# SwiGLU feed-forward on one core: the order of the first loads and of the first matrix products

## The chip, the cores and the metric

The kernel runs on one core of one Trainium2 chip. The metric is the device time of one execution in microseconds (us). Before the change three runs gave 120.45, 120.72 and 120.46 us, a median of 120.46 us. The engines of the core are named as in its profile: PE is the matrix engine (its weight loads have a lane of their own, PEld), ACT is ScalarE, DVE is VectorE, POOL is GpSimd, and SP is SyncE, which here only issues DMAs. A name with a q behind it (SPq, ACTq) is that engine's sequencer, which reads the engine's instructions in order and issues its DMAs.

## The reference

For 2048 tokens of width 512 and a hidden width of 1376, everything in bf16:

```
g = silu(x @ w_gate)      # x: 2048 x 512, w_gate: 512 x 1376
u = x @ w_up              # w_up: 512 x 1376
out = (g * u) @ w_down    # w_down: 1376 x 512
```

## The kernel before, in words

The tokens are cut into four chunks of 512 (`SC`), the hidden width into ten tiles of 128 columns and a last one of 96; such a tile is called an F tile here. The width of 512 is four slices of 128, over which each product is accumulated.

**What PE computes.** The products need x with its width on the partitions (`xT_sb`). For each chunk and F tile there are two groups of matmuls: a gate group (kind G) and an up group (kind U), each of four matmuls of 128 x 128 weights against 512 tokens, into a PSUM bank of its own. ACT reads the gate group's bank and writes silu of it, DVE multiplies that by the up group's bank and writes the hidden tile `hT_sb`. The odd last F tile is done in groups X and Y. When all chunks are done, groups of kind O multiply the hidden tiles by `w_down`, and the results are copied and stored. Groups use the eight PSUM banks in turn, in the order in which they are planned.

**The start.** x comes in by two ways. The first 256 tokens (`HT`) are loaded plainly into `xn_sb`, PE transposes them in eight transposes (four groups of kind T, line 346), and DVE and ACT each copy two of the four banks into `xT_sb`. The second 256 tokens of chunk 0, named `x0b`, come by a transposing DMA (line 87), as do chunks 1 to 3. Ahead of the transposes PE runs warming matmuls on constants (`warm`, line 337): `N_WARM` = 6 of 512 columns and `N_FILL` = 2 of 128 columns. They compute nothing.

Because x0b is late, the first groups are cut in two. PE runs the gate and the up group of F tiles 0 and 1 on the first 256 tokens (the very first two groups in steps of 128 tokens), and then the same four groups on the second 256 tokens. All later groups run on 512 tokens at once.

**The loads.** The weights come in slabs of F tiles (`slabs`): 0, 1, 2 to 3, 4 to 6, and 7 to the end; a slab is one DMA for gate and one for up (`load_w`, line 92). The two queues that issue them are ACT's and SP's. ACT issues gate 0 and up 0, and only then comes its first activation, on a dummy of 4 columns (line 269), ahead of which its table is loaded. SP issues, in this order, x's first half (line 108), gate 1, up 1, the transposing x0b, the slabs from F tile 2 on, a small piece of up (`wut`), the transposing loads of chunks 1 to 3, and the pieces of `w_down`. Each load has a semaphore of its own, and PE waits for it where it first needs the load (`need`). Each of the engines takes its instructions in the order written; PE's order is written out by hand in `on_tensor`.

Of the kernel before, what the change touches and what calls it, by code (L numbers as in the profile page):

```python
# [4 lines left out]
ACT = mybir.ActivationFunctionType  # L5
# [1 line left out]
BF16 = mybir.dt.bfloat16  # L7
FP32 = mybir.dt.float32

N_WARM = 6  # L10
N_FILL = 2


def bass_standalone__swiglu_ffn__prompt_kernel(nc, x, w_gate, w_up, w_down, out):
    _, S, D = x.shape
    F = w_gate.shape[1]
    P = 128
    KD = D // P
    NFF = F // P
    NFT = NFF + 1  # L20
# [8 lines left out]
    HT = SC // 2  # L29
# [10 lines left out]
    UPH = F + 32  # L40
# [4 lines left out]
    with ExitStack() as es:  # L45
# [12 lines left out]
        adummy = sb("act_dummy", [P, 8], FP32)  # L58
# [18 lines left out]
        def load_sem(name):  # L77
            loads[name] = sem(f"s_{name}")
            return loads[name]
# [3 lines left out]
        zero_c = nc.const_aps.tensor(0.0, [P, 4], FP32)  # L83


        def load_x(eng, name, t0, t1):
            eng.dma_start_transpose(
                xT_sb[:, :, t0:t1], xf[t0:t1, :]
            ).then_inc(load_sem(name), 16)

        def load_w(eng, name, src, base, f0, f1):
            eng.dma_start(
                w_sb[:, :, base + f0:base + f1],
                src[:, f0:f1].rearrange("(k p) f -> p k f", p=P),
            ).then_inc(load_sem(name), 16)

        slabs = [(0, 1), (1, 2), (2, 4), (4, 7), (7, NFT)]
        slab_of = {ft: a for a, b in slabs for ft in range(a, b)}

        def load_slab(eng, a, b):  # L100
            load_w(eng, f"wg{a}", w_gate, 0, a * P, min(b * P, F))
            load_w(eng, f"wu{a}", w_up, UPH, a * P, min(b * P, F - 32))

        def loads_on_scalar(act):
            load_slab(act, *slabs[0])

        def loads_on_sync(sp):
            sp.dma_start(
                xn_sb[:, :, :].rearrange("p j d -> p (j d)"), xf[0:HT, :].rearrange("(p j) d -> p (j d)", j=NXN)
            ).then_inc(load_sem("xn"), 16)  # L110
            load_slab(sp, *slabs[1])
            load_x(sp, "x0b", HT, SC)
            for a, b in slabs[2:]:
                load_slab(sp, a, b)
            load_w(sp, "wut", w_up, F - (F - 32), F - 32, F)
            for c in range(1, NSC):
                load_x(sp, f"x{c}", c * SC, (c + 1) * SC)
            sp.dma_start(
                wd_sb[:, 0:NFF, :], w_down[0:NFF * P, :].rearrange("(k p) d -> p k d", p=P)
            ).then_inc(load_sem("wd"), 16)  # L120
            for c in range(NSC):
                sp.dma_start(
                    wdt_sb[R * c:R * (c + 1), :, :], w_down[NFF * P:F, :].rearrange("(q p) d -> p q d", p=R)
                ).then_inc(load_sem(f"wdt{c}"), 16)
            sp.dma_start(wdl_sb[:, :], w_down[NFF * P:F, LASTA:D]).then_inc(load_sem("wdl"), 16)
# [3 lines left out]
        groups = []  # L129
# [3 lines left out]
        def add_group(kind, **what):  # L133
            g = dict(kind=kind, at=len(groups), bank=banks[len(groups) % NB], readers=[], **what)
            groups.append(g)
            return g
# [30 lines left out]
        def yblk(c):  # L167
            return (0, 64) if c % 2 == 0 else (64, 128)
# [39 lines left out]
        for i in range(NXN):  # L208
            for h, eng in enumerate("DA"):
                g = add_group("T", i=i, h=h)  # L210
                op = add_op(
                    eng, g, kind="copy", out=xT_sb[:, 2 * h:2 * h + 2, i * P:(i + 1) * P],
# [3 lines left out]
        NT = len(groups)  # L216
# [11 lines left out]
        for at in range(NST):  # L228
# [5 lines left out]
            for c0, c1 in halves:  # L234
                g = add_group("O", t=t, c0=c0, c1=c1, c=c)
                if c0 == 0:
                    quads[j].append(g)
                else:
# [3 lines left out]
                    eng, g, kind="copy", out=o_sb[ob][:, c0:c1], src=g["bank"][:, 0:c1 - c0],  # L242
# [22 lines left out]
            ).then_inc(s_I, 1)  # L265

        def on_scalar(act):
            loads_on_scalar(act)
            act.activation(adummy[:, 0:4], zero_c, ACT.Silu)  # L269
            for op in act_ops:  # L270
                act.wait_ge(s_P, op["g"]["at"] + 1)
                if op["kind"] == "silu":
                    if op["free"]:
                        act.wait_ge(s_D, op["free"])
                    fn = ACT.Silu
                else:
                    if op["stored"][1]:
                        act.wait_ge(*op["stored"])
                    fn = ACT.Copy
                act.activation(op["out"], op["src"], fn).then_inc(s_A, 1)  # L280
# [15 lines left out]
        def on_tensor(pe):  # L296
            landed = set()

            def need(name):
                if name not in landed:  # L300
                    pe.wait_ge(loads[name], 16)
                    landed.add(name)
# [3 lines left out]
            def after(eng, n):  # L306
                if n > read[eng]:
                    pe.wait_ge(s_A if eng == "A" else s_D, n)
                    read[eng] = n

            def free(g):
                if g["at"] >= NB:
                    for eng, n in groups[g["at"] - NB]["readers"]:
                        after(eng, n)

            def gu_matmuls(g, n0, n1):
                c, ft = g["c"], g["ft"]
                if c > 0:
                    need(f"x{c}")
                if c == 0 and n1 > HT:  # L320
                    need("x0b")
                need(("wg" if g["kind"] == "G" else "wu") + str(slab_of[ft]))
                col = (0 if g["kind"] == "G" else UPH) + ft * P
                for dk in range(KD):
                    if c == 0 and dk % 2 == 0:
                        for i in range(n0 // P, min(n1 // P, NXN)):
                            after(*xt_ready[i, dk // 2])
                    ins = pe.matmul(  # L328
                        g["bank"][:, n0:n1], lhsT=w_sb[:, dk, col:col + P],
                        rhs=xT_sb[:, dk, c * SC + n0:c * SC + n1], start=(dk == 0), stop=(dk == KD - 1),  # L330
                    )
                if n1 == SC:
                    ins.then_inc(s_P, 1)

            def warm(n, width):
                for i in range(n):
                    pe.matmul(banks[NB - 1][:, 0:width], lhsT=ones_w, rhs=ones_m[:, 0:width], start=True, stop=True)  # L337

            warm(N_WARM, SC)
            warm(N_FILL, P)  # L340
            pe.wait_ge(s_J, 1)
# [4 lines left out]
                    ins = pe.transpose(tview(g["bank"])[:, k, :], xn_sb[:, g["i"], dk * P:(dk + 1) * P], ident[:, :])  # L346
                ins.then_inc(s_P, 1)

            g0, u0, g1, u1 = groups[NT:NT + 4]
            for g in (g0, u0):  # L350
                gu_matmuls(g, 0, P)
                gu_matmuls(g, P, HT)
            gu_matmuls(g1, 0, HT)
            gu_matmuls(u1, 0, HT)
            for g in (g0, u0, g1, u1):
                gu_matmuls(g, HT, SC)

            for g in groups[NT + 4:]:
                kind = g["kind"]
                if kind == "O":  # L360
                    break
                free(g)
                if kind in "GU":
                    gu_matmuls(g, 0, SC)
                elif kind == "X":
                    c = g["c"]
                    need(f"wg{slab_of[NFF]}")
                    need("wut")
                    for dk in range(KD):
                        ins = pe.matmul(  # L370
                            g["bank"][:, :], lhsT=w_sb[:, dk, XC0:XC0 + P],
                            rhs=xT_sb[:, dk, c * SC:(c + 1) * SC],
                            start=(dk == 0), stop=(dk == KD - 1),
                        )
                    ins.then_inc(s_P, 1)
                elif kind == "Y":
                    need(f"wu{slab_of[NFF]}")
                    for dk in range(KD):
                        for c in (2 * g["pi"], 2 * g["pi"] + 1):
                            y0, y1 = yblk(c)  # L380
                            ins = pe.matmul(  # L381
                                g["bank"][y0:y1, :], lhsT=w_sb[:, dk, YC0:YC0 + 64],
                                rhs=xT_sb[:, dk, c * SC:(c + 1) * SC],
                                start=(dk == 0), stop=(dk == KD - 1),
                                tile_position=(0, y0), skip_group_check=True,
                            )
                    ins.then_inc(s_P, 1)
# [48 lines left out]
        on_sync(nc.sync)  # L436
        on_gpsimd(nc.gpsimd)
        on_scalar(nc.scalar)
        on_tensor(nc.tensor)
        on_vector(nc.vector)  # L440

# [27 lines left out]
```

## Time and profile before

| what | value |
|---|---|
| median of three runs | 120.46 us |
| the profiled execution, its own time | 120.32 us |
| its span | 118.9 us |
| PE busy | 115.4 us, 97% |
| PE weight loads busy | 54.1 us, 45% |
| DVE busy | 47.3 us, 40% |
| ACT busy | 31.0 us, 26% |
| moved by DMA | 8.84 MB |

Times in the trace count from the span's start. A row of the timeline gives an instruction's start and its duration, the engine, the line of the kernel, the operation, what it writes and reads, how many instructions were merged into the row, and in brackets how long the engine had been idle and what ended that. The row of a DMA on a sequencer (SPq, ACTq) is the issuing alone; when its data is there is told by the table of issues, which gives for each kind of DMA the time from the start of the issue to the landing.

### The profile page before, as it was taken

Reading aid. Unit: us, or ns where it says so; the run is one execution under the profiler, and the core shown is the slowest. Engines: PE = TensorE matmul, PEld = TensorE weight load, DVE = VectorE, ACT = ScalarE, POOL = GpSimd, SP = SyncE. Lnnn points to the kernel's source line nnn. Section 1 sums busy time; section 2 is a strip of 40 time slices with the busy share of each in tenths; the row PEclk is TensorE's granted clock in tenths of the full one; section 3 lists DMA queues with packets and bytes.
Section 4 is the critical chain, followed back from the end, with each engine's and each line's share of the span. In section 5 each row is a group of like instructions: output and inputs, shape, how many; then the busy total and the mean of one; then the engine's idle time right before and its main releaser. Section 6 shows DMA issues by size and latency. Waiting matters only on the chain.

```text
span 118.9 us, 1519 instructions
## 1 busy us (share of the span) xinstructions
PE 115.4 (97%) x600; PEld 54.1 (45%) x611; DVE 47.3 (40%) x73; ACT 31.0 (26%) x53; POOL 0.4 (0%) x5
## 2 busy tenths in 40 slices
PE   7999999999999999999999999999999999999993
PEld 2774444444444444444444444344434444444452
DVE  0133443353443444433444334469617422006530
ACT  4344324454234363244262343230000000000001
POOL 1000000000000000000000000000000000000000
PEclk9999999999999999999999999999999999999999
DMA  3999999970000000000000000000004221002412
GB/s 103 271 307 357 264 162 242 328 183 24 0 0 0 6 0 0 0 3 3 0 0 0 6 0 0 0 0 0 0 0 138 88 88 44 0 0 75 145 50 88
DMA packets 17559, 8.84 MB, mean 74 GB/s; under 512 B 10640, under 2 KB 17424, under 8 KB 17552
## 3 DMA queue, kind: packets, MB, share of 16 engines
q1 hardware_dynamic: 16496, 8.48, 26.7%
q10 hardware_dynamic: 1056, 0.26, 1.0%
q8 instruction: 5, 0.08, 0.3%
q14 instruction: 2, 0.02, 0.1%
HBM read 4.81 MB, written 2.10 MB: 58 GB/s over the span
## 4 chain that ended last, share of the span: by engine, by line
PE 97%; issue 1%; DVE 0%
PE bank L328 58%; PE bank L394 29%; PE bank L370 3%; PE bank L337 2%; PE bank L408 2%; PE bank L381 2%; PE bank L346 1%; DVE o_sb L293 0%; PE bank L431 0%
## 5 line engine op out<-in xcount | busy, mean ns | idle before, releaser
L328 PE MATMUL bank<-xT_sb,w_sb 128*128 128x512 bf16 (+2 forms) x338 | 69.7, 364 | 0.4
L328 PEld LDWEIGHTS bank<-xT_sb,w_sb 128*128 128x128 bf16 x344 | 32.8, 98 | 36.4 <-issue 0.2
L289 DVE TENSOR_TENSOR hT_sb<-sg_sb,bank 128x512 bf16<-128x512 f32 x40 | 27.5, 688 | 40.5 <-PE bank L328 36.6
L394 PE MATMUL bank<-wd_sb,hT_sb 128*128 128x512 bf16 (+2 forms) x166 | 34.5, 366 | 0.4 <-issue 0.3
L280 ACT ACTIVATE sg_sb<-bank 128x512 f32<-128x512 f32 x40 | 23.8, 596 | 40.8 <-PE bank L328 40.8
L394 PEld LDWEIGHTS bank<-wd_sb,hT_sb 128*128 128x128 bf16 x170 | 16.1, 98 | 19.1 <-issue 1.3
L293 DVE CAST o_sb<-bank 128x512 bf16<-128x512 f32 (+1 forms) x16 | 10.1, 663 | 22.0 <-PE bank L408 12.3
L280 ACT ACTIVATE o_sb<-bank 128x384 bf16<-128x384 f32 x1 | 0.5, 492 | 37.8 <-PE bank L394 37.8
L289 DVE TENSOR_TENSOR ht_sb<-sgy_sb,bank 32x512 bf16<-32x512 f32 x8 | 5.5, 684 | 0.2
L289 DVE TENSOR_TENSOR ht_sb<-sgx_sb,bank 32x512 bf16<-32x512 f32 x4 | 2.8, 691 | 3.5 <-ACT sgx_sb L280 3.5
L370 PE MATMUL bank<-xT_sb,w_sb 128*128 128x512 bf16 x15 | 4.1, 379 | 0.1
L337 PE MATMUL bank<-const-bfloat16-1.0 128*128 128x512 bf16 (+1 forms) x8 | 2.9, 545 | 0.8 <-PEq L454 0.8
L280 ACT ACTIVATE sgx_sb<-bank 32x512 f32<-32x512 f32 x4 | 2.4, 588 | 4.5 <-PE bank L370 4.5
L408 PE MATMUL bank<-wdt_sb,ht_sb 32*128 32x512 bf16 (+1 forms) x48 | 2.9, 372 | 0.0
L370 PEld LDWEIGHTS bank<-xT_sb,w_sb 128*128 128x128 bf16 x16 | 1.6, 98 | 1.9
L280 ACT ACTIVATE sgy_sb<-bank 64x512 f32<-64x512 f32 x4 | 2.4, 590 | 0.1
L337 PEld LDWEIGHTS bank<-const-bfloat16-1.0 128*128 128x128 bf16 x8 | 1.0, 136 | 2.4 <-issue 2.4
L381 PE MATMUL bank<-xT_sb,w_sb 128*64 128x512 bf16 x16 | 1.9, 382 | 0.0
L408 PEld LDWEIGHTS bank<-wdt_sb,ht_sb 32*128 32x128 bf16 x48 | 1.1, 93 | 1.7 <-issue 0.8
L269 ACT ACT_TABLE_LOAD x1 | 1.3, 1283 | 1.8 <-issue 1.8
L293 DVE COPY xT_sb<-bank 128x256 bf16<-128x256 bf16 x2 | 0.6, 292 | 2.7 <-PE bank L346 2.7
L381 PEld LDWEIGHTS bank<-xT_sb,w_sb 128*64 128x64 bf16 x16 | 0.8, 109 | 1.0 <-DVE hT_sb L289 0.4
(14 smaller groups left out, 4.0 us busy)
## 6 DMA issues: line engine op xcount, KB each, us to landing
out_dram<-o_sb SPq DMA_DIRECT2D x15, 128.0 KB, 1.7
wd_sb<-in_w_down_dram SPq DMA_DIRECT2D x1, 1280.0 KB, 9.2
w_sb<-in_w_gate_dram SPq DMA_DIRECT2D x1, 480.0 KB, 5.9
w_sb<-in_w_up_dram SPq DMA_DIRECT2D x1, 448.0 KB, 6.5
w_sb<-in_w_gate_dram SPq DMA_DIRECT2D x1, 384.0 KB, 4.5
w_sb<-in_w_up_dram SPq DMA_DIRECT2D x1, 384.0 KB, 5.1
wdt_sb<-in_w_down_dram SPq DMA_DIRECT2D x4, 96.0 KB, 7.5
xn_sb<-in_x_dram SPq DMA_DIRECT2D x1, 256.0 KB, 2.8
```

Source lines behind the costliest of these rows:

```text
L269: act.activation(adummy[:, 0:4], zero_c, ACT.Silu)
L280: act.activation(op["out"], op["src"], fn).then_inc(s_A, 1)
L289: ins = dve.tensor_tensor(op["out"], op["a"], op["b"], ALU.mult)
L293: ins = dve.tensor_copy(op["out"], op["src"])
L328: ins = pe.matmul(g["bank"][:, n0:n1], lhsT=w_sb[:, dk, col:col + P], rhs=xT_sb[:, dk, c * SC + n0:c * SC + n1], start=(dk == 0), stop=(dk ...
L337: pe.matmul(banks[NB - 1][:, 0:width], lhsT=ones_w, rhs=ones_m[:, 0:width], start=True, stop=True)
L346: ins = pe.transpose(tview(g["bank"])[:, k, :], xn_sb[:, g["i"], dk * P:(dk + 1) * P], ident[:, :])
L370: ins = pe.matmul(g["bank"][:, :], lhsT=w_sb[:, dk, XC0:XC0 + P], rhs=xT_sb[:, dk, c * SC:(c + 1) * SC], start=(dk == 0), stop=(dk == KD - 1),
L381: ins = pe.matmul(g["bank"][y0:y1, :], lhsT=w_sb[:, dk, YC0:YC0 + 64], rhs=xT_sb[:, dk, c * SC:(c + 1) * SC], start=(dk == 0), stop=(dk == ...
L394: ins = pe.matmul(g["bank"][:, 0:c1 - c0], lhsT=hT_sb[:, fk, t * P:(t + 1) * P], rhs=wd_sb[:, fk, c0:c1], start=(start and fk == 0), stop= ...
L408: ins = pe.matmul(g["bank"][:, 0:c1 - c0], lhsT=ht_sb[R * c:R * (c + 1), q, j * P:(j + 1) * P], rhs=wdt_sb[R * c:R * (c + 1), q, c0:c1], s ...
```

## The change

- ACT's dummy activation, and with it the load of its table, now stands ahead of ACT's DMAs. ACT then issues up 0, up 1, gate 2 and up 2 (four DMAs of 128 KB each).
- SP issues x's first half, gate 0, gate 1, the transposing x0b, and then the slabs from F tile 3 on. It issues as many DMAs as before.
- The slabs are 0, 1, 2, 3 to 4, 5 to 7, 8 to the end.
- `N_EARLY` = 3: the groups of F tiles 0, 1 and 2 run on the first 256 tokens, then all six on the second 256. The third tile's groups are planned as ninth and tenth behind the four transposing groups and so use banks 0 and 1 again; PE waits with `free` for the copies that read them.
- One warming matmul of 512 columns less (`N_WARM` 5).

```diff
-N_WARM = 6
+N_WARM = 5
 N_FILL = 2
+N_EARLY = 3
...
-        slabs = [(0, 1), (1, 2), (2, 4), (4, 7), (7, NFT)]
+        slabs = [(0, 1), (1, 2), (2, 3), (3, 5), (5, 8), (8, NFT)]
...
         def loads_on_scalar(act):
-            load_slab(act, *slabs[0])
+            load_w(act, "wu0", w_up, UPH, 0, P)
+            load_w(act, "wu1", w_up, UPH, P, 2 * P)
+            load_slab(act, *slabs[2])
 
         def loads_on_sync(sp):
...
-            load_slab(sp, *slabs[1])
+            load_w(sp, "wg0", w_gate, 0, 0, P)
+            load_w(sp, "wg1", w_gate, 0, P, 2 * P)
             load_x(sp, "x0b", HT, SC)
-            for a, b in slabs[2:]:
+            for a, b in slabs[3:]:
                 load_slab(sp, a, b)
...
         def on_scalar(act):
+            act.activation(adummy[:, 0:4], zero_c, ACT.Silu)
             loads_on_scalar(act)
-            act.activation(adummy[:, 0:4], zero_c, ACT.Silu)
...
-            g0, u0, g1, u1 = groups[NT:NT + 4]
-            for g in (g0, u0):
-                gu_matmuls(g, 0, P)
-                gu_matmuls(g, P, HT)
-            gu_matmuls(g1, 0, HT)
-            gu_matmuls(u1, 0, HT)
-            for g in (g0, u0, g1, u1):
+            early = groups[NT:NT + 2 * N_EARLY]
+            for i, g in enumerate(early):
+                free(g)
+                if i < 2:
+                    gu_matmuls(g, 0, P)
+                    gu_matmuls(g, P, HT)
+                else:
+                    gu_matmuls(g, 0, HT)
+            for g in early:
                 gu_matmuls(g, HT, SC)
 
-            for g in groups[NT + 4:]:
+            for g in groups[NT + 2 * N_EARLY:]:
```

## The prediction

> **What bounds the kernel now.** I read the page first: the busy shares, then the chain that ended last.
>
> ```profile
> span 118.9 us, 1519 instructions
> PE 115.4 (97%) x600; PEld 54.1 (45%) x611; DVE 47.3 (40%) x73; ACT 31.0 (26%) x53; POOL 0.4 (0%) x5
> ...
> PE 97%; issue 1%; DVE 0%
> ```
>
> The chain of waits is PE's own work from 0.77 us to the end. Nothing in this change alters the arithmetic, so only the head can move: how early PE does useful work, and what it waits for until about 10 us. A delay there goes through to the end whole, because PE never idles later. So next I read the timeline of the first 10 us.
>
> ```profile
> 0.73 0.46 ACTq L92 DMA_DIRECT2D w_sb<-in_w_gate_dram  x1
> 0.74 0.40 SPq L108 DMA_DIRECT2D xn_sb<-in_x_dram  x1
> 0.77 2.93 PE L337 MATMUL bank<-const-bfloat16-1.0 128*128 128x512 bf16 x8 [0.77 <-PEq L454]
> ...
> 1.20 0.41 SPq L92 DMA_DIRECT2D w_sb<-in_w_gate_dram  x1
> 1.22 0.53 ACTq L92 DMA_DIRECT2D w_sb<-in_w_up_dram  x1
> ...
> 1.66 0.50 SPq L92 DMA_DIRECT2D w_sb<-in_w_up_dram  x1
> 1.78 1.28 ACT L269 ACT_TABLE_LOAD   x1 [1.78 <-issue]
> ...
> 2.20 1.69 SPq L87 DMA_TRANSPOSE xT_sb<-in_x_dram  x1
> ...
> 3.08 0.20 ACT L269 ACTIVATE act_dummy<-const-float32-0.0 128x4 f32<-128x4 f32 x1
> 3.29 0.15 PEld L337 LDWEIGHTS bank<-const-bfloat16-1.0 128*128 128x128 bf16 x1 [0.28 <-issue]
> 3.60 0.63 PEld L346 LDWEIGHTS bank<-ident,xn_sb 128*128 128x128 bf16 x8 [0.16 <-issue]
> ...
> 4.44 1.81 PEld L328 LDWEIGHTS bank<-xT_sb,w_sb 128*128 128x128 bf16 x24 [0.21 <-issue]
> ...
> 6.42 7.47 PEld L328 LDWEIGHTS bank<-xT_sb,w_sb 128*128 128x128 bf16 x44 [0.17 <-DMA xT_sb<-in_x_dram]
> ```
>
> The weight loads show the starts of PE's steps: transposes at 3.60, gate 0 at 4.44, the second 256 tokens at 6.42. Only the last start is put down to a DMA. Third, the table of issues, for when each load is there:
>
> ```profile
> xn_sb<-in_x_dram SPq DMA_DIRECT2D x1, 256.0 KB, 2.8
> ...
> w_sb<-in_w_gate_dram ACTq DMA_DIRECT2D x1, 128.0 KB, 3.2
> w_sb<-in_w_gate_dram SPq DMA_DIRECT2D x1, 128.0 KB, 3.4
> w_sb<-in_w_up_dram ACTq DMA_DIRECT2D x1, 128.0 KB, 3.7
> w_sb<-in_w_up_dram SPq DMA_DIRECT2D x1, 128.0 KB, 3.7
> ```
>
> Start of issue plus time to landing: x 0.74 + 2.8 = 3.5; gate 0 0.73 + 3.2 = 3.9; gate 1 1.20 + 3.4 = 4.6; up 0 1.22 + 3.7 = 4.9; up 1 1.66 + 3.7 = 5.3; x0b 2.20 + 4.2 = 6.4 (4.2 is its own row). PE's weight loads first need them at 4.44 (gate 0), 5.00 (up 0), 5.45 (gate 1), 5.83 (up 1), 6.27 (x0b). So x ends the warming, up 0 is 0.1 us ahead of its use, and x0b is 0.1 us behind.
>
> **The change part by part.**
>
> *One warming matmul less.* Warming weight loads come 0.43 us apart (the last at 2.86 and 3.29), so the warming ends at about 3.12 instead of 3.55. What is late next is x, which lands at 3.5. The packets tell what can move it: x's first packets run from 1.78 us and its last ends at 3.15; ACT's gate 0 joins from 2.50 and from there x's last third crawls. Afterwards up 0 joins in gate 0's place if ACT issues at once. Then x lands at 3.4 to 3.5, and the 0.43 us turn into waiting: gain 0, at the best 0.1. If ACT issues late, x has the engines to itself, would end near 2.65 at its first rate (60 KB per 0.2 us) and land near 3.0.
>
> *Does ACT issue at once?* No row of before has a DMA behind an ACT activation. The nearest: ACT's sequencer passed a semaphore instruction at 23.07, 0.01 us after the activation at 23.06 began, with another (23.67) still queued between; it runs ahead of its engine. POOL too starts instructions of 0.10 us each 0.03 us apart. The table load itself could be an exception. Bounds for ACT's first DMA: 0.8 and 0.73 + 1.28 + 0.20 = 2.2. I take 0.8, the rows that show a sequencer at work.
>
> [...]
>
> *Gate 0 moves behind x on SP.* It takes gate 1's place in the queue (1.20), with ACT's queue beside it as then: landing 4.6 instead of 3.9, needed 4.44. Gate 0's first load moves to about 4.62. Part comes back: before, its eight loads took 5.00 - 4.44 = 0.56 us, since the copies of the transposes ended up to 4.88; at 0.056 us each they need 0.45. So up 0 starts at 5.07 instead of 5.00: **+0.07**.
>
> *Up 0, gate 1, up 1.* Up 0 takes gate 0's place in ACT's queue (3.9 to 4.0, needed 5.07): hidden behind gate 0. Up 1 takes up 0's place (4.9 to 5.0, needed 5.95): hidden behind gate 1's matmuls. Gate 1 takes up 1's place on SP: 5.3, needed 5.52; but ACT's queue, empty from 4.5 us before, now carries 256 KB more through that time. Bounds 0 and 0.15 (half of the rate for the last 66 KB at some 55 KB per 0.2 us); nearest to the row of 5.3, I take **+0.05**.
>
> *F tile 2 from ACT, 256 tokens first.* Gate 2 and up 2 are issued at about 1.9 and 2.4, against 3.94 and 4.56 from SP before (landed 7.2 and 8.0). A half group of four matmuls takes 4 x 0.109 = 0.437 us, so PE's needs are now: up 0 5.07, gate 1 5.57, up 1 6.01, gate 2 6.44, up 2 6.88, x0b 7.32. By bytes, at 260 KB per us from 1.78 and 0.4 us to the signal, x, six weight tiles and x0b (1280 KB) are all there at 1.78 + 4.92 + 0.4 = 7.1; gate 2 earlier, about 6.0; up 2 6.6 to 6.9. I take no wait; bounds 0 and +0.25, if up 2 or x0b is last of them. Running tile 2 in halves costs 16 matmuls of 0.109 in place of 8 of 0.216: **+0.02**. The wait for x0b goes: the loads at 6.157 and 8.074 enclose 17 steps, 1.92 us where 17 x 0.109 = 1.86: **-0.06**. Banks 0 and 1 were copied out by 4.88: free.
>
> *ACT's table* is loaded by 2.2 instead of 3.28 and needed at 4.22: hidden both ways. *SP's later queue:* as many issues at the same places; slab 3 to 4 has the same 1536 KB through it as before through up 2 (8.0), needed at 9.8: hidden.
>
> *The sum:* 0 + 0.07 + 0.05 + 0.02 - 0.06 = +0.08 us. The profiled execution took 120.32 us (span 118.9, 1.4 around it), 0.14 under the median 120.46. So 120.40 for a like profile and **120.54** as a median.
>
> **The rivals.** Some 0.3% (0.36 us) is what a measurement here can tell from no change.
>
> *ACT's queue is held by the table load (slower).* Its DMAs start at 2.2: up 0 lands at 2.2 + 3.2 to 3.7 = 5.4 to 5.9, and up 2, issued at about 3.9, by the bytes ahead of it (with slab 3 to 4 beside it) between 7.0 and 8.0. PE takes up 2 last of the early groups: 0.44 for it and 24 x 0.109 = 2.62 for the second halves, so the next tile starts at 10.1 to 11.1 instead of 9.69: +0.4 to +1.4, middle 0.9: 121.4. It decides as soon as ACT's first DMA starts later than about 1.4 us, which brings up 0 behind 5.07. For it: no row shows a DMA behind a table load. Against it: the sequencer that runs ahead.
>
> *The clock rises later (slower).* Eight transposes run at 0.107 apart until 4.0 and 0.056 after; the granted clock's record starts at 4.02, 3.27 us after the first warming matmul. A gap of 0.4 us at 3.12 is new. If the count began again at 3.5, the clock would rise at 6.8, and 2.2 us of matmuls from 4.6 on would run at half speed: +1.1, 121.6. Against it: 2.9 of those 3.27 us stay busy.
>
> [...]
>
> *x is really earlier (faster).* If x lands at 3.0 and gate 0 right behind it at 4.0, and up 0 still by 4.75, transposes start 0.43 earlier; cold they take longer (eight at 0.107), so up 0 starts about 0.28 earlier. With the wait for x0b and the splitting: -0.32; with nothing lost, -0.43 - 0.06 + 0.02 = -0.47. 120.0 to 120.15. It needs ACT's loads out of x's way and yet early, between the two bounds.
>
> **How the numbers follow.** No wait by ACT, the sum above: 0.41, of which 0.05 lie above +0.36 (both upper bounds, 0.15 + 0.25, met). ACT held: 0.31. Clock: 0.09. x earlier: 0.19, of which 0.03 and the small gains stay within 0.3%, 0.16 beyond it. So faster 0.16, same 0.39, slower 0.45. The likeliest single case is the sum, own range 120.3 to 120.9. The range over the cases reaches from the fast case's 120.0 to 121.5, inside the held queue's +0.4 to +1.4; above it and below it about 0.2 are left.
>
> **What would show it.** ACT's first DMA at about 0.8 beside its table load (right), or behind 2.0 (held). The warming ending at 3.1 and the first transpose at 3.5 (right) or 3.1 (x earlier). Gate 0's first load at 4.6, put down to the DMA of w_sb. No wait for x0b ahead of the second halves at 7.3 to 7.5. The next tile (line 328, 512 tokens) at 9.8. Matmuls of 128 columns 0.056 apart from 4.6 on; at 0.107 the clock was late. Everything behind it shifted evenly; if the end moves by another amount than the third tile's end, the prediction is wrong in a place that I took as untouched.

## The result

The changed kernel takes 121.2 us (median of 121.05 to 121.38, four runs) against 120.45 for the kernel before (120.35 to 120.72, four runs beside it): a ratio of 1.0053, with a 95% interval of 1.0027 to 1.0078. It is slower, by half a per cent. The profiled execution took 121.05 us with a span of 119.7. The ratios here and below leave out executions more than 1.5% above the fastest of their kernel (three, in one experiment), and they are not quotients of the medians shown, from which they differ by up to 0.14%.

From here on "tile 2" is F tile 2, "gate 2" and "up 2" its two loads, and "landed" means the start of the issue plus the time to landing, counted from the span's start.

### The profile page after: what moved, and what is told of

It reads as the page before. It is cut to its first block, busy times and chain, and to the rows that moved or that the text cites. A ratio compares the mean times of both kernels' runs of the same rounds, so it can differ in the third digit from the quotient of the medians.

```text
span 119.7 us, 1535 instructions
## 1 busy us (share of the span) xinstructions
PE 116.0 (97%) x607; PEld 55.5 (46%) x618; DVE 47.3 (39%) x73; ACT 31.1 (26%) x53; POOL 0.4 (0%) x5
## 4 chain that ended last, share of the span: by engine, by line
PE 94%; DMA 3%; issue 1%; SPq 0%; DVE 0%
PE bank L332 58%; PE bank L400 29%; DMA w_sb<-in_w_gate_dram 3%; PE bank L376 3%; PE bank L414 2%; PE bank L387 2%; SPq L111 0%; DVE o_sb L297 0%; PE bank L437 0%
## 5 line engine op out<-in xcount | busy, mean ns | idle before, releaser
L332 PEld LDWEIGHTS bank<-xT_sb,w_sb 128*128 128x128 bf16 x352 | 34.3, 100 | 35.6 <-DMA w_sb<-in_w_gate_dram 0.3
L376 PEld LDWEIGHTS bank<-xT_sb,w_sb 128*128 128x128 bf16 x16 | 1.6, 98 | 1.9
L350 PE MATMUL bank<-ident,xn_sb 128*128 128x128 bf16 x8 | 1.0, 308 | 0.4 <-DMA xn_sb<-in_x_dram 0.4
```

Source lines behind the costliest of these rows:

```text
L332: ins = pe.matmul(g["bank"][:, n0:n1], lhsT=w_sb[:, dk, col:col + P], rhs=xT_sb[:, dk, c * SC + n0:c * SC + n1], start=(dk == 0), stop=(dk ...
L376: ins = pe.matmul(g["bank"][:, :], lhsT=w_sb[:, dk, XC0:XC0 + P], rhs=xT_sb[:, dk, c * SC:(c + 1) * SC], start=(dk == 0), stop=(dk == KD - 1),
```

## The profile after

ACT and SP in the first 3 us of the changed kernel (timeline: start, duration, engine, line, operation):

```profile
0.73 1.28 ACT L272 ACT_TABLE_LOAD   x1 [0.73 <-PEq L460]
0.74 0.39 SPq L111 DMA_DIRECT2D xn_sb<-in_x_dram  x1
...
0.79 1.01 ACTq L93 DMA_DIRECT2D w_sb<-in_w_up_dram  x2
...
1.19 0.97 SPq L93 DMA_DIRECT2D w_sb<-in_w_gate_dram  x2
...
1.83 0.53 ACTq L93 DMA_DIRECT2D w_sb<-in_w_gate_dram  x1
...
2.20 1.80 SPq L88 DMA_TRANSPOSE xT_sb<-in_x_dram  x1
...
2.39 0.53 ACTq L93 DMA_DIRECT2D w_sb<-in_w_up_dram  x1
```

ACT's sequencer issues its DMAs beside the table load, from 0.79 us on, not behind it. PE's weight loads in the same execution:

```profile
3.60 0.78 PEld L350 LDWEIGHTS bank<-ident,xn_sb 128*128 128x128 bf16 x8 [0.59 <-issue]
...
4.72 6.28 PEld L332 LDWEIGHTS bank<-xT_sb,w_sb 128*128 128x128 bf16 x59 [0.35 <-DMA w_sb<-in_w_gate_dram]
```

The transposes start at 3.60, exactly as before: x landed at 3.49 again, and the dropped warming matmul became waiting. Gate 0 starts at 4.72 instead of 4.44. Tile 3's second weight load, which starts with its first matmul, stands at 9.91 in the profile before and at 10.69 here, 0.78 later. The end moved by about as much (0.81, span 118.92 to 119.72), so the whole loss lies in the head.

Two things differ in that head, and this pair of profiles cannot tell them apart. First the loads: gate 2 landed at 6.37, up 2 at 7.57 and x0b at 7.78, where x0b had landed at 6.38. The issues of the changed kernel up to 4.5 us (KB each, median us to landing):

```profile
w_sb<-in_w_up_dram ACTq DMA_DIRECT2D x3, 128.0 KB, 3.7
...
w_sb<-in_w_gate_dram ACTq DMA_DIRECT2D x1, 128.0 KB, 4.5
xT_sb<-in_x_dram SPq DMA_TRANSPOSE x1, 5.6
```

x0b took 5.6 us from its issue, against 4.2 before. (The row of three up loads has a median of 3.7, but the third of them, up 2, took 5.2.) Second, PE's clock: the matmuls of 128 columns ran 0.107 us apart until 6.1 us, where before they came 0.056 apart from 4.0 on. The groups of PE between 4.7 and 6.1 us show it in the mean of 307 ns, against 220 ns in the profile before:

```profile
L332 PE MATMUL bank<-xT_sb,w_sb 128*128 128x128 bf16 x14 | 1.6, 307 | 0.1
```

## The experiments

Three theories stood at the start. *Clock*: the shorter warming leaves a gap in PE's work, which puts the clock's rise off. *Loads*: tile 2's loads from ACT come ahead of or beside x0b, and PE, which takes its groups in a fixed order, waits for up 2. *Gate*: gate 0's late landing on SP is the loss.

### The warming put back

```diff
-N_WARM = 5
+N_WARM = 6        # in the changed kernel
```

> The changed kernel with its sixth warming matmul put back; all else as changed. Three theories stand. CLOCK: the shorter warming leaves PE idle from 3.1 to 3.6 us, which puts the rise of its clock off from 4.0 to about 6.1, and that is the whole +0.75. LOADS: four loads ahead of x0b on ACT's queue and three on SP's make up 2 land at 7.6, so the second halves cannot begin before about 8.0; that alone is worth +0.7, and the slow clock lies beside it. GATE: gate 0 lands at 4.68 behind x on SP instead of 3.93, and that shift is the loss. Clock expects 120.6: matmuls 0.056 apart from 4.0 on and 0.55 to 0.6 saved. Loads expects about 121.1: matmuls 0.056 apart from 4.0 on, but then a wait of about 0.65 for up 2 from 6.95 to 7.6, and the next tile no earlier than 10.6. Gate expects 121.2, unchanged.

Measured: 121.12 us against 120.61, ratio 1.0033 (1.0010 to 1.0057). The loss stays. The profiled execution took 121.59 and shows the slow clock until 6.2 us although the gap was closed, so in this execution it was late without a gap. PE's weight loads, with the wait that the Loads theory needs:

```profile
4.60 2.84 PEld L332 LDWEIGHTS bank<-xT_sb,w_sb 128*128 128x128 bf16 x28 [0.26 <-DMA w_sb<-in_w_gate_dram]
8.15 1.86 PEld L332 LDWEIGHTS bank<-xT_sb,w_sb 128*128 128x128 bf16 x18 [0.71 <-DMA w_sb<-in_w_up_dram]
```

PE waits 0.71 us for up 2, which landed at 8.11.

### The shorter warming alone

```diff
-N_WARM = 6
+N_WARM = 5        # in the kernel before
```

> The kernel before with one warming matmul less and nothing else. Clock expects PE's matmuls of 128 columns to stay 0.107 apart until about 6, gate 1 at 6.1 to 6.2 instead of 5.45, the wait for x0b gone, and 121.0 to 121.1. Loads and Gate expect no change, 120.45, since x lands at 3.5 as before.

Measured: 120.53 against 120.61, ratio 1.0001 (0.9976 to 1.0025). The ten executions lie between 120.21 and 121.29, those of the kernel before beside it between 120.23 and 121.24: the same spread with the same lower end. If the gap always put the clock off, none could have taken 120.21. The Clock theory falls, as far as it ties the clock to the warming.

### Tile 2 back on SP

```diff
-N_WARM = 5
-N_EARLY = 3
+N_WARM = 6
+N_EARLY = 2
-            load_slab(act, *slabs[2])
...
-            for a, b in slabs[3:]:
+            for a, b in slabs[2:]:
```

> The changed kernel with six warming matmuls, F tile 2 loaded by SP behind x0b and run on 512 tokens (N_EARLY 2); the table first, and gate 0 and gate 1 on SP, up 0 and up 1 on ACT, stay. Loads expects x0b back near 6.4 and 120.45 to 120.6, what is left being gate 0's late landing (0.07 to 0.28). Gate expects most of the loss to stay: 120.9 to 121.2. Clock expects 120.5, as for any kernel with six warming matmuls.

Measured: 120.76 against 120.61, ratio 1.0003 (0.9979 to 1.0026). x0b landed at 6.45. The table first, gate 0 and gate 1 on SP and up 0 and up 1 on ACT cost nothing that these runs can tell. The Gate theory falls, and the loss is bound to what was taken out: tile 2 on ACT and its early groups.

### Tile 2 on ACT, gate 0 early

```diff
-            load_w(act, "wu0", w_up, UPH, 0, P)
-            load_w(act, "wu1", w_up, UPH, P, 2 * P)
+            load_slab(act, *slabs[0])
             load_slab(act, *slabs[2])
...
-            load_w(sp, "wg0", w_gate, 0, 0, P)
-            load_w(sp, "wg1", w_gate, 0, P, 2 * P)
+            load_slab(sp, *slabs[1])     # and N_WARM 6
```

> Six warming matmuls, table first, ACT issues gate 0, up 0, gate 2 and up 2, SP issues x, gate 1, up 1, x0b: so gate 0 is early and the clock in time, and only tile 2's loads from ACT with its half groups ahead of x0b are left of the change. Loads expects up 2 near 7.6 and x0b near 7.8 and about 121.1. Clock and Gate expect 120.45.

Measured: 121.05 against 120.61, ratio 1.0025 (1.0007 to 1.0043). Here the clock rose at 4.7 and gate 0 landed at 3.96, and the loss is there nevertheless. PE's weight loads:

```profile
5.15 1.76 PEld L330 LDWEIGHTS bank<-xT_sb,w_sb 128*128 128x128 bf16 x22 [0.19 <-ACT xT_sb L282]
7.42 0.66 PEld L330 LDWEIGHTS bank<-xT_sb,w_sb 128*128 128x128 bf16 x7 [0.52 <-DMA w_sb<-in_w_up_dram]
```

PE is ready for up 2 at 6.9 and waits until 7.42 (up 2 landed at 7.38). This is the Loads theory's wait, by itself.

### The two halves of it: loads alone, order alone

The loads of the change with PE's order of before:

```diff
-N_WARM = 5
-N_EARLY = 3
+N_WARM = 6
+N_EARLY = 2
```

> The changed kernel's loads (table first; up 0, up 1, gate 2 and up 2 from ACT; gate 0, gate 1, x0b from SP) with six warming matmuls and PE's order of before, two tiles early. What is open is which half of the loss belongs to the loads and which to PE's order. If the 256 KB of tile 2 ahead of x0b are a cost in themselves, x0b lands at 7.6 to 7.8 as in the changed kernel, PE waits for it from about 6.4, the next tile after the third starts at 11.2 instead of 9.9, and the time is 121.6 to 121.9, worse than the change. If the order alone (up 2 ahead of the second halves) is the cost, 120.6.

Measured: 121.9 against 120.5, ratio 1.0120 (1.0089 to 1.0151). The last of PE's waits:

```profile
7.96 2.94 PEld L332 LDWEIGHTS bank<-xT_sb,w_sb 128*128 128x128 bf16 x23 [1.27 <-DMA xT_sb<-in_x_dram]
```

And the order of the change with tile 2 from SP behind x0b:

```diff
-N_WARM = 5
+N_WARM = 6
-            load_slab(act, *slabs[2])
...
-            for a, b in slabs[3:]:
+            for a, b in slabs[2:]:
```

> The other half: six warming matmuls, tile 2 loaded by SP behind x0b (x0b near 6.4 as before), but three tiles run early, so PE takes up 2 ahead of the second halves. If the order is a cost in itself, PE waits for gate 2 (about 7.1) and up 2 (about 7.7) while x0b lies there since 6.4, the second halves start near 8.2, and the time is 121.2 to 121.7. If only the loads cost, 120.6.

Measured: 121.11 against 120.5, ratio 1.0047 (1.0025 to 1.0070), a little under what the order theory expected. The two waits:

```profile
6.95 0.33 PEld L331 LDWEIGHTS bank<-xT_sb,w_sb 128*128 128x128 bf16 x4 [0.45 <-DMA w_sb<-in_w_gate_dram]
7.49 3.60 PEld L331 LDWEIGHTS bank<-xT_sb,w_sb 128*128 128x128 bf16 x32 [0.21 <-DMA w_sb<-in_w_up_dram]
```

x0b lay there from 6.45, but PE's order asks for gate 2 (6.90) and up 2 (7.45) first. Each half is a loss by itself. Together (1.0033, the run with the warming put back) they lose less than the loads alone (1.0120): the third tile's early groups hide most of x0b's delay, and what is left is the wait for up 2.

### The kernel before, once more

> The kernel before, unchanged, profiled once more. The profiles so far have PE's clock rising at 4.0 (before), 6.1 (changed), 6.1 (six warming matmuls put back), 4.7, 5.5 and 6.6, with no regard to the warming. If that rise differs from execution to execution of one program, this one will have it at another place than 4.02, anywhere from 4 to 7.4, and its time goes with it: about 120.3 plus 0.36 for each us that the rise is later. If the rise belongs to the program, it is 4.0 again and 120.3.

The kernel is that of before, unchanged. Measured: 121.13 us, where the profile before took 120.32. PE's groups between 4.5 and 6.4 us, first of the profile before, then of this one:

```profile
L328 PE MATMUL bank<-xT_sb,w_sb 128*128 128x128 bf16 x16 | 1.2, 220 | 0.1
```

```profile
L328 PE MATMUL bank<-xT_sb,w_sb 128*128 128x128 bf16 x16 | 1.9, 308 | 0.0
```

The same 16 matmuls ran slower (308 ns each against 220), and the first of 256 columns behind them at half the rate (6.22 to 6.44, 0.21 us where it takes 0.11 later), until about 6.5 us. Tile 3's first load came at 10.48 instead of 9.69, 0.79 later; the time is 0.81 longer. So the clock's rise wanders between executions of one program: 4.0 and 6.5 in the kernel before, 6.8 with its warming shortened, 4.6 to 6.2 in the others shown here up to this point. That 7.4 is the latest, as the expectation has it, is shown by no run; in the next one the rise was at 9.9. The chip of the first profile is not on record, but on the chip of the second alone 19 executions of this kernel spread from 120.20 to 121.14.

### x0b right behind x

```diff
-N_EARLY = 3
+N_EARLY = 1
-            load_w(act, "wu0", w_up, UPH, 0, P)
-            load_w(act, "wu1", w_up, UPH, P, 2 * P)
-            load_slab(act, *slabs[2])
+            load_slab(act, *slabs[0])
+            load_slab(act, *slabs[1])
...
-            load_w(sp, "wg0", w_gate, 0, 0, P)
-            load_w(sp, "wg1", w_gate, 0, P, 2 * P)
...
-            for a, b in slabs[3:]:
+            for a, b in slabs[2:]:       # N_WARM 6, slabs of before
```

> An attempt at a version better than both: x0b is issued by SP right behind x; ACT loads its table first and then issues gate 0, up 0, gate 1, up 1; tile 2 comes from SP as before; only tile 0 runs early on 256 tokens (N_EARLY 1), then its second halves, then whole tiles. By the bytes, x0b would land by 6, ahead of its need at about 5.4 to 6.2. Loads expects PE to wait 0 to 0.5 for x0b, and gains of 0.06 (x0b's wait of before) and 0.02 (eight split matmuls fewer) if it lands in time: 120.4 to 120.9, against about 120.5.

Measured: 121.33 against 120.5, ratio 1.0064 (1.0043 to 1.0085): worse than the kernel before and no better than the change (1.0053). x0b landed at 6.08, hardly earlier for its place in the queue, and up 0, now beside it, at 6.19 instead of 4.9:

```profile
6.23 2.69 PEld L329 LDWEIGHTS bank<-xT_sb,w_sb 128*128 128x128 bf16 x18 [0.91 <-DMA w_sb<-in_w_up_dram]
```

In this profiled execution, of 123.13 us, the clock rose only at 9.9; three of eleven executions took 123.1 to 123.3. That a wait of 0.91 us causes this was not tried, and the landings and the wait shown are those of this one execution.

### Half the dose

```diff
-N_WARM = 5
-N_EARLY = 3
+N_WARM = 6
+N_EARLY = 2
-            load_slab(act, *slabs[2])
+            load_w(act, "wg2", w_gate, 0, 2 * P, 3 * P)
...
+            load_w(sp, "wu2", w_up, UPH, 2 * P, 3 * P)
             for a, b in slabs[3:]:
```

> Half the dose of the run with tile 2's loads alone: ACT issues up 0, up 1 and gate 2, and up 2 goes to SP behind x0b; six warming matmuls, two tiles early. With none of tile 2 on ACT x0b landed at 6.45 and the time was within 0.1 of the kernel before; with both halves, 256 KB, at 7.92 and 121.9. If x0b's landing goes by the bytes ahead of it, 128 KB bring it to 7.1 to 7.3 and the time to 121.1 to 121.3. If it goes by the number of queued loads on ACT or by the second of them alone, x0b stays near 6.5 or goes to 7.9.

Measured: 121.08 against 120.5, ratio 1.0034 (1.0018 to 1.0051). x0b landed at 6.98, a little ahead of the 7.1 to 7.3 expected, and PE's last wait is

```profile
7.03 4.02 PEld L333 LDWEIGHTS bank<-xT_sb,w_sb 128*128 128x128 bf16 x28 [0.33 <-DMA xT_sb<-in_x_dram]
```

So 0, 128 and 256 KB of tile 2 on ACT put x0b at 6.45, 6.98 and 7.92. At the 280 GB/s that the profile before shows between 5.0 and 5.6 us, 128 KB take 0.47 us (an estimate): the first step, 0.53, is near that, the second, 0.94, is twice as long.

### Up 1 on ACT

```diff
-N_EARLY = 3
+N_EARLY = 2
-            load_w(act, "wu0", w_up, UPH, 0, P)
+            load_slab(act, *slabs[0])
             load_w(act, "wu1", w_up, UPH, P, 2 * P)
-            load_slab(act, *slabs[2])
...
-            load_w(sp, "wg0", w_gate, 0, 0, P)
...
-            for a, b in slabs[3:]:
+            for a, b in slabs[2:]:       # N_WARM 6, slabs of before
```

> A second attempt at a version better than both: ACT loads its table first, then issues gate 0, up 0 and up 1; SP issues x, gate 1, and x0b one place earlier (at 1.7 instead of 2.2); slabs, six warming matmuls and two early tiles as before. The same 768 KB stand ahead of x0b or beside it, so x0b should land at 6.2 to 6.4 and PE's wait for it, 0.06 at the most, go: 120.4 to 120.5 against 120.5, the same within 0.3%. If an earlier place in its queue is worth as much as the bytes, x0b lands by 5.9 and up 1 at 5.9 to 6.2, and PE waits for up 1 instead: 120.5 to 120.8.

Measured: 121.51 against 120.5, ratio 1.0073 (1.0048 to 1.0099). Both guesses were wrong. With not one byte more ahead of x0b than in the kernel before, x0b landed at 7.36 and up 1 at 7.57 (5.33 before). PE's wait, and two rows of the stretches of time (us, the busy time of each engine, the clock, the DMA engines' busy share, GB/s; the clock column reads 1.00 here although PE's matmuls of 128 columns stand 0.107 us apart until 6.1, so in this document the clock is read from their spacing):

```profile
7.61 3.38 PEld L330 LDWEIGHTS bank<-xT_sb,w_sb 128*128 128x128 bf16 x27 [0.98 <-DMA w_sb<-in_w_up_dram]
```

```profile
4.40:5.00 0.60, 0.60 (x8) 0.43 (x7) 0.29 (x1) 0.56 (x2) 0.00 (x0) 1.00 1.34 192
5.00:5.60 0.60, 0.60 (x9) 0.52 (x7) 0.00 (x0) 0.10 (x1) 0.00 (x0) 1.00 1.01 172
```

In the profile before the same two stretches moved 287 and 280 GB/s. The amount ahead of x0b is not the whole of it: up 1, from ACT's queue and beside x0b, ended late itself (7.57). The run changed two things, up 1's queue and x0b's place, and does not say which of them brought the low rate.

### Tile 2 ahead of x0b, but on SP

```diff
             load_slab(act, *slabs[0])
-            load_slab(act, *slabs[2])    # against the run "gate 0 early" above
...
             load_slab(sp, *slabs[1])
+            load_slab(sp, *slabs[2])
             load_x(sp, "x0b", HT, SC)
```

> As the run with gate 0 first and tile 2 on ACT (121.05; up 2 landed at 7.38, x0b at 7.62), with one difference: gate 2 and up 2 are issued by SP, ahead of x0b, so the same 256 KB stand ahead of x0b, but no other queue carries loads while the transposing load runs. Three tiles early, six warming matmuls. If the bytes ahead are all that counts, up 2 and x0b land where they did, PE waits for up 2, and the time is 121.0. If running beside the transposing load is what costs (up 1 on ACT beside x0b landed at 7.57 with no more bytes ahead than before), up 2 lands at 6.3 to 6.6, ahead of its need at about 6.9, x0b at 7.2 to 7.5, near its need at 7.3, and the time is 120.4 to 120.7.

Measured: 120.62 against 120.46, ratio 1.0016 (0.9996 to 1.0035): no loss that is clear of no change, with the same 256 KB ahead of x0b and the same PE order as in the run "gate 0 early". The ratios of the two (1.0016 and 1.0025) are not clear of each other, but the lower ends differ: nine of the twelve executions here lie below 120.85, the lowest of the ten there, down to 120.32. The two ran on different chips, where the kernel before went down to 120.30 and 120.23. And the trace is plain. Gate 2 landed at 5.88, up 2 at 6.33 (7.38 there), x0b at 7.45 (7.62), and among PE's weight loads up to 10.9 us none has an idle time put down to a DMA:

```profile
4.58 0.48 PEld L330 LDWEIGHTS bank<-xT_sb,w_sb 128*128 128x128 bf16 x6
5.25 5.69 PEld L330 LDWEIGHTS bank<-xT_sb,w_sb 128*128 128x128 bf16 x55 [0.19 <-ACT xT_sb L282]
```

So it is seen how up 2 is delayed. On ACT's queue, tile 2's packets run interleaved with x0b's: between 5.9 and 6.5 us each of the two queues starts 26 to 30 KB in every 0.2 us. The two end together, ACT's last packet at 6.78 and x0b's near 6.84, where PE needs up 2 first. On SP's queue they go one after the other: up 2's last packet ends at 5.77, x0b's packets follow. SP's issues in this run:

```profile
2.75 0.51 SPq L93 DMA_DIRECT2D w_sb<-in_w_up_dram  x1
3.30 2.05 SPq L88 DMA_TRANSPOSE xT_sb<-in_x_dram  x1
```

The bytes moved between 4.4 and 6.2 us are nearly the same in both (283, 281 and 272 GB/s against 288, 287 and 272 by thirds). One thing these two runs do not part: with two more issues ahead of it on SP, x0b is also issued later (3.30 against 2.21), and tile 2 on ACT with x0b held back by as much was not run.

### The changed kernel, once more

> The changed kernel, unchanged, profiled once more. The clock's rise differs between executions of one program (4.0 and 6.2 in two profiles of the kernel before, 120.32 and 121.13). If PE's early groups are bound by up 2's landing from ACT's queue, the time hardly goes with the rise: where the clock rises by 5, PE waits 0.4 to 0.6 for up 2 and the time is 120.9 to 121.1; where it rises at 6 or later, the wait is 0.1 to 0.3 and the time 121.0 to 121.4. If up 2 bound nothing, an early rise would give about 120.5.

Measured: 120.99 us, beside 120.48 for the kernel before. The clock rose at 4.4, in spite of the gap in the warming, and PE's weight loads show the waits that a late clock hides:

```profile
4.53 1.13 PEld L332 LDWEIGHTS bank<-xT_sb,w_sb 128*128 128x128 bf16 x16
5.91 1.21 PEld L332 LDWEIGHTS bank<-xT_sb,w_sb 128*128 128x128 bf16 x12 [0.25 <-DMA w_sb<-in_w_gate_dram]
7.56 3.39 PEld L332 LDWEIGHTS bank<-xT_sb,w_sb 128*128 128x128 bf16 x31 [0.45 <-DMA w_sb<-in_w_up_dram]
```

With an early clock the weight loads wait 0.25 for gate 1 (landed 5.86) and 0.45 for up 2 (7.52), and the time is 120.99. The matmuls, a step behind their loads, lose 0.24 and 0.34. Against the profile before, gate 1's first matmul would come 0.17 later without its wait (x landed 0.08 later, the clock rose 0.36 later); with the two waits, 0.05 less for x0b and 0.02 more for the split matmuls, that makes 0.72, and tile 3's second load is 0.72 later (10.63 against 9.91), the time 0.67. With a late clock, in the first profile, PE computes slowly meanwhile (matmuls 0.107 apart until 6.1); they lose nothing to gate 1 and 0.03 to up 2 (they start at 7.49, 7.62 and 7.74, where the step is 0.11), and the time is 121.05. So the change takes away the executions near 120.3: none of its five lies under 120.99, none of the ten with the warming put back under 120.97. The two late ones look alike: 121.13 for the kernel before (the rise that the expectation puts at 6.2 was at 6.5), 121.05 for the changed one.

## Why the prediction was right or wrong

The time lies inside the stated range of 120.0 to 121.5, but the likeliest case, 120.54, did not come about, and that the range held the time is luck. With both upper bounds of the sum it is 120.9; the range reached to 121.5 for a held ACT queue, which did not happen. Slower was given 0.45, of which 0.40 stood for that and for the clock; what happened, late loads, had the 0.05 of the upper bounds.

- **One warming matmul less, gain 0.** Right. x landed at 3.49, and the time went into waiting. The shorter warming alone measured 1.0001.
- **ACT issues at once.** Right: 0.79, predicted 0.8, beside the table load. The rival of a held queue falls with it, and so does its sum by the bounds.
- **Gate 0 behind x on SP, +0.07.** Landed at 4.68 in the first profile and 4.47 in the second (predicted 4.6). With the rest of the reordered loads it cannot be told from no change (1.0003).
- **Gate 1, +0.05 between 0 and 0.15.** Undersized: landed at 5.42 in the first profile, but at 5.86 in the second, where the matmuls lost 0.24.
- **Tile 2 from ACT, "I take no wait; bounds 0 and +0.25".** This is the step that failed. It let the loads land in the order of their need, up 2 at 6.6 to 6.9 and x0b at 7.1. They landed at 7.57 and 7.78. The packets were nearly where the sum had them (the last end at 6.9, the sum gave 6.7); two things were wrong. The sum took up 2 to end ahead of x0b, but on two queues they ended together (6.91 and 6.90). And it took 0.4 us from the last packet to the signal, the row of the kernel before (ACT's last packet at 4.52, landed 4.87); beside x0b it was 0.66 for up 2 and 0.88 for x0b. The weight loads' wait for up 2 was 0.45 in the change's second profile, 0.52 with gate 0 early and 0.71 with the warming put back, and the next tile, forecast at 9.8, came at 10.5 to 10.6.
- **The wait for x0b goes, -0.06.** It went, and a larger one took its place one step earlier in PE's order.
- **The clock rises later, +1.1.** The first profile looked like this rival come true, with matmuls 0.107 apart until 6.1, and it was not: the rise came at 4.0 and at 6.5 us in two profiles of the kernel before, with the same warming. No run shows a count that begins again behind a gap, from which the rival had its 6.8: with the gap the rise came at 6.1 and 4.4 in the two profiles of the change and at 6.8 in that of the kernel before. Nor was its price right: a rise 2.5 us later cost the kernel before 0.81, where the sum had 1.1 for 2.2. (The clock's record starts 3.24 us after the first warming matmul; the 3.27 counts from its weight load.)
- **0.3% as the measurement's grain.** Too fine. Executions of the kernel before lie between 120.20 and 121.24, 0.9%, and the two that were profiled, 120.32 and 121.13, differ by their clock. With some ten executions the interval is still 0.17 to 0.25% to either side.
- **x really earlier.** Did not come about: x landed between 3.46 and 3.71 in all profiles. ACT's first load was issued by 0.80 us in each of them, so the case's condition, ACT's loads out of x's way, was never met.

No version here beats the kernel before. Behind the transposes its matmuls lost 0.05 us to a load (x0b: matmuls at 6.26 and 6.42, 0.16 apart instead of 0.11), so there was next to nothing for the new order of loads to gain.

## What to carry to other kernels

When an in-order engine waits for several loads, put them in the order of need on one queue. Here the packets of two queues ran interleaved, so the load needed first ended with the one needed last (6.91 and 6.90 us in the change), and splitting loads over a second idle queue lost more (1.0120) than a third early tile could hide (1.0033 were left). With tile 2 on ACT PE's weight loads waited 0.52 us for up 2, and with it on SP, and x0b issued behind it, not at all, though the two ratios (1.0025 and 1.0016) are not clear of each other. When a head is bound by loads, add up not just the bytes but which load ends when, and do not take the time from the last packet to the signal from another moment: it was 0.35 us for up 0 in the profile before, and 0.66 and 0.88 beside x0b in the change. And before two profiles are compared, look for what differs between executions of one program (here 120.32 and 121.13 us, by the clock's rise); a second profile of the unchanged kernel is the cheapest way.

## What the runs showed of the hardware

- ScalarE's sequencer issued DMAs while its table loaded: the first at 0.79 us beside a load from 0.73 to 2.01.
- The clock's rise came at 4.0 to 6.8 us in thirteen of the fourteen profiles, whatever the warming, and at 9.9 in one with a wait of 0.91 us before it. Each microsecond later cost the kernel before about 0.3 us (0.81 over 2.5).
- The time from the last packet to the landing was 0.33 to 0.47 us for ACT's loads that ended before x0b's packets began, and 0.59 to 1.08 for those that ended beside x0b's packets or within 0.2 us of their end. The run with x0b right behind x has three that fit neither: 0.40 for gate 0, beside the first of x0b's packets, and 0.88 and 0.54 for two loads that ended 1 and 2 us behind the last.
- Beside x0b's transposing load, the DMA engines' rate fell to 172 and 192 GB/s with up 1 on ACT and to 162 GB/s between 5.6 and 6.2 us in the run with the warming put back, but stayed at 214 GB/s and more in the others, by stretches of 0.6 us. What sets off such a stretch stays open.
